# One fused attention and feed-forward kernel: the bias tables built in another way, the last tile's activations in other buffers, and every engine's queue in a new order

## The chip, the core and the metric

The kernel runs on one core of one Trainium2 chip. A core has five engines that work side by side and meet at semaphores: TensorE (PE in the profile; PEld is its weight load), VectorE (DVE), ScalarE (ACT), GpSimd (POOL) and SyncE (SP), and 16 DMA engines that move data. The metric is the time of one execution on the device in microseconds (us), as the median of several executions. Less is better.

## The reference

Attention with a bias by distance, over 8 batches, 8 heads, 576 positions and 64 channels a head, and a feed-forward layer with a leaky ReLU behind it:

```python
scores = scale * np.matmul(q, k.transpose(0, 1, 3, 2))      # 8, 8, 576, 576
bias = bias_table[bucket]                                   # 32 buckets by |i - j|, one row of 8 heads each
attn = softmax(scores + bias)                               # over the last axis
x = (attn @ v), heads side by side: 4608 rows of 512
h = x @ w_in                                                # 512 -> 2048
g = np.maximum(0.01 * h, h)
out = g @ w_out                                             # 2048 -> 512, float32
```

The bucket of a distance is the distance itself below 16, then grows with its logarithm, and is the last of the 32 from distance 128 on.

## The kernel before

**Attention.** The unit is a pair of heads of one batch, `n` = 0 to 31 (4 pairs in each of 8 batches). For a pair, q and k are turned so that channels lie on partitions (by PE from `rows`, L415 to L438, for the first pairs, later by a DMA transpose that SP issues, L424, into `tu`), and copied into `qt` and `kt` (L447). `score` (L472 to L480) multiplies them, 64 partitions a head or 128 for the leftover blocks; `expo` on ACT (L499 to L510) takes the exponential out of PSUM into `at`; `band` on DVE (L523) multiplies the band of |i - j| < 128 + 64 or so by a table of exponentials of the bias; `av` (L552, L555) multiplies by v with a column of ones, so that the row sums come with it; `norm` (L562 to L570) divides, and the result is turned back into `xT` (L576 by DMA, L584 and L589 by PE and a copy).

**The bias tables.** The exponential of the bias less that of the last bucket is a function of i - j and the head. `hk` holds it, skewed over partitions. It is made at the program's start: `hot` is a one-hot map, 32 partitions (one a bucket) by 512 distances, put together by DVE copies out of the identity matrix (L344 to L352), of which each constant run of a bucket is one copy (L348). Three more copies, each shifted by one column, stand on the other three groups of 32 partitions (`hots`, L358). `shift_table` (L361) takes the last bucket off the bias on PE, `exp_table` (L366) puts the exponentials block by block into `diag` in four ACT operations. `spread` (L374) is 16 small matmuls for each of 6 parts of the table, and `take_spread` (L377) copies each part into `hk`; `make_hk4` (L381) makes the copy for the leftover blocks. The rows of k for pair 0 come by a DMA of their own into `raw` (in the tile `y`), and ACT casts them into `pr` (L420) in one operation.

**Feed-forward.** Tokens are taken in 9 tiles `T` of 512. Tiles 0 to 2 run plain products (`ffn_in`, L603, 16 of them a tile); tiles 3 to 8 and all output products use a scheme of seven block products in place of eight. In it the input side has four units `u` a tile, each with seven products (`in_product`, L651), copies and additions into `stage` (L656 on ACT or DVE, L661 on DVE), and activations (`in_act`, L592 on ACT) that write `g`, which is [128, 16, 512] and holds one tile. `mix_g` (L687, DVE) forms sums and differences of blocks of `g`: into `gs` and, in place, into `g`. `product` (L715) is the output side, seven products of two halves `ts`, 8 matmuls each. `out_take` (L723) and `out_add` (L728) put them together in `y`, and SP stores it (L737).

There is one `g`, so the activations of a tile wait until the output products of the tile before have read it (`free_g` in `plan_seven`). In the last tile, in the order of the PE queue, products 1 and 2 are followed by product 6, which reads the block that `mix_g` 1 changes: one DVE operation over all 2048 columns.

**What sets the order.** Every step is a task with a number (`add`). `Plan.QUEUES` lists, for each engine, the numbers in the order in which they are issued, and `BANKS` the PSUM bank of each; an engine works through its own list in order and waits wherever the data is not there. Which of ACT and DVE does a copy is given by the list in which its number stands (`mover`). `FILL` puts idle matmuls on scratch data (`spin`, L1177) ahead of some tasks on PE; ten more stand at the program's start. SP and POOL issue DMAs in the order of their lists; POOL's loads of q, k, v and the weights wait for the readers of the buffer.

## Time and profile before

| | |
|---|---|
| time, median of 3 executions | 353.74 us (353.22 to 355.13) |
| the profiled execution | 354.99 us, of which the span from the first to the last instruction is 353.2 us |
| PE busy | 345.5 us, 98% of the span |
| PEld busy | 257.8 us, 73% |
| DVE busy | 298.8 us, 85% |
| ACT busy | 283.2 us, 80% |
| POOL busy | 69.4 us, 20% |
| granted TensorE clock | 1.000 mean |

How to read the lines that follow in the prediction. A row of the timeline is: start in us, duration in us, engine, line of the kernel, operation, output tile <- input tiles, partitions x elements and type, count of such instructions in a row, and in brackets the idle time of the engine just before with what ended it. Matmuls overlap, so a matmul's duration is longer than the distance to the next one; rows of the chain (the work that ended last, followed back) give the distance instead. A row of the windows gives, for a stretch of time, its length and for each engine the busy time with the number of instructions, then the granted clock, the busy share of the DMA engines and GB/s. A row of the groups gives the group, xcount, busy us, mean ns of one, and the idle time before.

### The profile page before, as it was taken

How to read it: one execution, taken by the hardware profiler on the slowest of the kernel's cores; microseconds unless marked ns; L12 is line 12 of the kernel's file. 1: busy time of each engine (PE TensorE's matmuls, PEld its weight loads, DVE VectorE, ACT ScalarE, POOL GpSimd, SP SyncE). 2: the span in 40 equal slices, each digit the busy share in tenths (PEclk: the TensorE clock that was granted, in tenths of full speed). 3: DMA queues.
4: the chain of work that ended last, by engine and by line, in shares of the span. 5: the costliest groups of instructions: out<-in, count | busy, mean ns of one | idle time of the engine just before them, and what ended most of it. 6: DMA issues, size and time to landing. Idle time of an engine off the chain costs nothing.

```text
span 353.2 us, 10334 instructions
## 1 busy us (share of the span) xinstructions
PE 345.5 (98%) x4365; PEld 257.8 (73%) x4365; DVE 298.8 (85%) x646; ACT 283.2 (80%) x436; POOL 69.4 (20%) x107
## 2 busy tenths in 40 slices
PE   8899999999999999999999999999999999999996
PEld 5666458865577556777887778688877888888875
DVE  6998599967799578998999999989988998587871
ACT  5998989589987888997987999999977981682841
...
GB/s 126 148 190 199 207 194 166 50 149 155 181 113 145 166 171 85 139 115 151 131 130 127 80 164 89 53 128 113 40 2 40 76 65 0 81 42 1 121 30 91
DMA packets 102542, 39.32 MB, mean 111 GB/s; under 512 B 82016, under 2 KB 97376, under 8 KB 102496
## 3 DMA queue, kind: packets, MB, share of 16 engines
...
q10 hardware_dynamic: 208, 0.29, 0.3%
q14 instruction: 12, 0.10, 0.1%
...
## 4 chain that ended last, share of the span: by engine, by line
PE 90%; DMA 4%; DVE 4%; ACT 1%; issue 0%; DVEq 0%; ACTq 0%
PE ps L715 29%; PE ps L651 20%; PE ps L603 12%; PE ps L552 11%; PE ps L472 9%; DMA tu<-pr 4%; PE ps L479 2%; PE ps L1177 2%; PE ps L539 1%; PE ps L492 1%; ACT g L592 1%; PE ps L433 1%; PE ps L584 1%; PE ps L438 1%; DVE g L687 1%; DVE hk L381 1%
## 5 line engine op out<-in xcount | busy, mean ns | idle before, releaser
L499 ACT ACTIVATE at<-ps 128x1024 bf16<-128x1024 f32 x124 | 123.8, 1036 | 13.1 <-PE ps L472 12.3
L715 PEld LDWEIGHTS <-g 128*128 128x128 bf16 x864 | 82.0, 98 | 16.3 <-issue 5.4
L523 DVE TENSOR_TENSOR at<-at,hk 128x768 bf16<-128x768 bf16 (+4 forms) x156 | 65.6, 447 | 9.9 <-ACT at L510 5.1
L293 POOL DMA_DIRECT2D vn<-in_v_dram x32 | 28.9, 915 | 133.6 <-PE ps L552 121.6
L715 PE MATMUL ps<-mix,g 128*128 128x256 bf16 x432 | 53.5, 273 | 0.6 <-DVE g L687 0.6
L715 PE MATMUL ps<-w_out_sb,g 128*128 128x256 bf16 x432 | 52.8, 273 | 0.0
L661 DVE TENSOR_TENSOR stage<-ps,stage 128x512 f32<-128x512 f32 x72 | 47.8, 684 | 4.8 <-PE ps L651 3.9
L552 PEld LDWEIGHTS <-at 128*128 128x128 bf16 x1240 | 42.1, 98 | 6.1 <-issue 3.5
L552 PE MATMUL ps<-vn,at 128*128 128x65 bf16 x1240 | 45.6, 194 | 0.3 <-DVE opair L563 0.3
L592 ACT ACTIVATE g<-stage 128x512 bf16<-128x512 f32 x72 | 42.5, 636 | 4.1 <-DVE stage L661 2.2
L592 ACT ACTIVATE g<-ps 128x512 bf16<-128x512 f32 x72 | 41.9, 613 | 4.0 <-PE ps L603 2.6
L603 PE MATMUL ps<-xT,w_in_sb 128*128 128x512 bf16 x192 | 45.1, 379 | 0.0
L472 PE MATMUL ps<-qt,kt 64*128 64x512 bf16 x256 | 42.8, 385 | 1.2 <-DVE qt L447 1.2
L651 PEld LDWEIGHTS <-w_in_sb 128*128 128x128 bf16 x384 | 36.0, 98 | 7.5 <-issue 2.8
L723 ACT COPY y<-ps 128x512 f32<-128x512 f32 x33 | 19.6, 594 | 23.7 <-PE ps L715 23.6
L656 ACT COPY stage<-ps 128x512 f32<-128x512 f32 x48 | 27.6, 592 | 9.9 <-PE ps L651 9.6
L603 PEld LDWEIGHTS <-w_in_sb 128*128 128x128 bf16 x192 | 17.2, 98 | 20.6 <-issue 2.4
L651 PEld LDWEIGHTS <-early 128*128 128x128 bf16 x288 | 27.2, 98 | 6.2 <-issue 2.7
L728 DVE TENSOR_TENSOR y<-ps,y 128x512 f32<-128x512 f32 (+1 forms) x29 | 18.7, 648 | 10.9 <-PE ps L715 6.0
L651 PE MATMUL ps<-early 128*128 128x256 bf16 x192 | 27.4, 273 | 0.0
L651 PE MATMUL ps<-early,w_in_sb 128*128 128x256 bf16 x192 | 27.3, 273 | 0.0
L651 PE MATMUL ps<-xT,w_in_sb 128*128 128x256 bf16 x192 | 26.7, 273 | 0.0
(107 smaller groups left out, 461.2 us busy)
## 6 DMA issues: line engine op xcount, KB each, us to landing
out_dram<-y SPq DMA_DIRECT2D x16, 512.0 KB, 3.5
...
```

The costliest lines, as they stand in the source:

```text
L293: nc.gpsimd.dma_start(out=vn[i][:, c, :, 0:D], in_=v[b, :, c * P : (c + 1) * P, :].rearrange("h s d -> s h d"),)
L472: nc.tensor.matmul(ps[:, e, :], lhsT=kt[r, u * P : (u + 1) * P], rhs=qt[r, 0:512], start=True, stop=True)
L499: nc.scalar.activation(at[:, :, u, 0:512], ps, AF.Exp, scale=scale)
L523: nc.vector.tensor_tensor(out=o, in0=o, in1=m, op=ALU.mult)
L552: nc.tensor.matmul(ps[:, ic, :], lhsT=at[:, o : o + P], rhs=vn[i][:, c, 2 * p + e, :], start=whole and c == 0, stop=not whole and ic == NJ ...
L592: nc.scalar.activation(out_, in_, AF.Prelu, bias=0.0, scale=1.0, alpha=0.01)
L603: nc.tensor.matmul(bank(("in", T, f))[:, o : o + n], lhsT=w_in_sb[:, c, f * P : (f + 1) * P], rhs=xT[:, c, x : x + n], start=(c == 0 and i ...
L651: nc.tensor.matmul(ps[:, j, :], lhsT=l, rhs=r, start=first and j == 0 and c == 0, stop=k in (2, 4, 3) and j == 1 and c == KH - 1, skip_gro ...
L656: copy(out=stage[u % 2][:, s], in_=ps)
L661: nc.vector.tensor_tensor(out=st, in0=ps, in1=st, op=ALU.add)
L715: nc.tensor.matmul(ps, lhsT=l[:, ts * P : (ts + 1) * P], rhs=r, start=k in (1, 2, 5) and (split or ts == 0) and j == 0, stop=k in (4, 2, 3 ...
L723: copy(out=y_block(k), in_=bank(("a", T)).rearrange("p (s e) -> p s e", s=2))
```

## The change

Three things change.

**The tables.** `diag` is no longer cleared and filled block by block: ACT takes one exponential over all 128 partitions into a small float32 table (`exp_table`), and DVE multiplies it by a 0/1 map of the groups (`make_diag`); the map, and the column that tells the last bucket's rows, come from two DVE reductions over the identity matrix. The far part of the one-hot map is one ACT copy over all four groups instead of DVE's 512-wide copy; the three longest runs go to ACT too. The shifted copies shrink from 511, 510 and 509 columns to 263 each and become tasks of their own (`shift_hot`), which may stand on DVE or ACT and anywhere in the queue. The cast of pair 0's raw k is split in two halves of 384 (`raw_rows`), one of which stands on ACT and one on DVE.

**The last tile.** The activations of tile 8 go into two buffers of the attention, free by then (`at_`, 8 of 16 blocks each), and wait no longer for tile 7's output products. `mix_g` 1 and 3 of that tile are split in two halves.

**The queues.** All lists in `QUEUES` and `BANKS` are new, and `FILL` holds 8 idle matmuls in place of 23.

The numbers of the tasks shift by up to seven, since there are new ones. Here the program's start on DVE, from the last runs of the one-hot map to the first copies for pair 1, before:

```order
L348 COPY stage_78<-ident 32x2x14
L348 COPY stage_78<-ident 32x2x16
L352 COPY stage_78<-stage_78 32x15
L358 COPY stage_78<-stage_78 32x511
L358 COPY stage_78<-stage_78 32x510
L358 COPY stage_78<-stage_78 32x509
L447 COPY kt_89<-ps 128x576
L451 TENSOR_TENSOR kt_89<-kt_89,own 128x128
L377 CAST hk<-ps 128x8x64 x4
L447 COPY kt_90<-ps 128x576
```

And the same place after (the changed file's lines L359, L368, L377, L398, L471 and L475 are L348, L352, L358, L377, L447 and L451 of before; L444 is half of the cast of raw k):

```order
L359 COPY stage_78<-ident 32x2x11
L367 COPY stage_78<-ident 32x16
L368 COPY stage_78<-stage_78 32x15
L373 TENSOR_REDUCE flat<-ident 128x4
L386 TENSOR_TENSOR diag<-flat 128x32
L377 COPY stage_78<-stage_78 32x263
L444 CAST pr_95<-y 96x384
L377 COPY stage_78<-stage_78 32x263 x2
L398 CAST hk<-ps 128x8x64 x4
L475 TENSOR_TENSOR kt_89<-kt_89,own 128x128
L471 COPY qt_93<-ps 128x576
```

The first copy into `kt` is gone from DVE here; it stands on ACT, behind that into `qt`. Half of the cast stands between the shifted copies.

The end of DVE's queue, tile 8, before (L687 is `mix_g`, L661 an addition of the input side, L728 one of the output side):

```order
L687 TENSOR_TENSOR gs<-g 128x1024
L661 TENSOR_TENSOR stage_78<-ps,stage_78 128x512
L661 TENSOR_TENSOR stage_77<-ps,stage_77 128x512
L661 TENSOR_TENSOR stage_78<-ps,stage_78 128x512
L687 TENSOR_TENSOR g<-g 128x4x256
L687 TENSOR_TENSOR gs<-g 128x1024
L687 TENSOR_TENSOR g<-g 128x4x256
L687 TENSOR_TENSOR g<-gs,g 128x8x256
L728 TENSOR_TENSOR y<-ps,y 128x2x256
L687 TENSOR_TENSOR g<-g 128x8x256
L728 TENSOR_TENSOR y<-ps,y 128x256 x4
```

And after, where L720 is `mix_g` and L764 `out_add`:

```order
L685 TENSOR_TENSOR stage_78<-ps,stage_78 128x512
L720 TENSOR_TENSOR at_104<-at_104 128x4x256
L720 TENSOR_TENSOR gs<-at_105 128x1024
L720 TENSOR_TENSOR at_105<-at_105 128x4x256
L720 TENSOR_TENSOR at_104<-gs,at_104 128x4x256
L720 TENSOR_TENSOR at_105<-gs,at_105 128x4x256
L764 TENSOR_TENSOR y<-ps,y 128x2x256
L720 TENSOR_TENSOR at_104<-at_104 128x4x256
L720 TENSOR_TENSOR at_105<-at_105 128x4x256
L764 TENSOR_TENSOR y<-ps,y 128x256 x4
```

The two operations over 2048 columns are now two over half of them, each on a buffer of its own.

The end of ACT's queue, from the last but four activations of tile 8 (L592) to the copies of output products (L723), before:

```order
L592 ACTIVATE g<-stage_77 128x2x256
L592 ACTIVATE g<-ps 128x2x256 x2
L592 ACTIVATE g<-stage_78 128x2x256
L592 ACTIVATE g<-stage_77 128x2x256
L592 ACTIVATE g<-stage_78 128x2x256
L723 COPY y<-ps 128x2x256 x4
```

And after (L616 and L759):

```order
L616 ACTIVATE at_105<-stage_77 128x2x256
L616 ACTIVATE at_105<-stage_78 128x2x256
L616 ACTIVATE at_105<-ps 128x2x256
L616 ACTIVATE at_105<-stage_77 128x2x256
L616 ACTIVATE at_105<-stage_78 128x2x256
L759 COPY y<-ps 128x2x256 x5
```

There are five copies where there were four: the copy of product 4 of tile 7 stands behind the first one of tile 8, because on PE both halves of that product (16 matmuls) now stand behind the last input product of tile 8. Before, they stood ahead of the last 72 matmuls of tile 8's input side.

The code's core:

```diff
     QUEUES = {
         "PE": """
-            0 18 17 27 39 37 33 31 25 47 60 61 41 43 29 23 45 90 89 68 119 66 72 76 74 105 118 97 99 95 70 54 56 103 155
...
+            0 19 20 34 28 44 48 32 36 42 65 66 95 46 30 73 94 75 38 52 106 50 110 124 79 71 123 100 81 77 59 102 61 104
...
-    FILL = {18: 5, 27: 2, 72: 1, 74: 4, 105: 5, 95: 1, 70: 5}
+    FILL = {19: 6, 50: 1, 77: 1}
...
     diag = per.tile([P, G, H], BF16, name="diag")
-    nc.vector.memset(diag, 0.0)
     hots = tables.bitcast(BF16)[:, 2 * G * NB : 2 * G * NB + UW]
     hot = hots[0:NB, :]
-    nc.vector.tensor_copy(out=hot, in_=ident[0:NB, NB - 1 : NB].to_broadcast([NB, UW]))
-    nc.vector.tensor_copy(out=hot[:, C0 : C0 + small], in_=ident[0:NB, 0:small])
+    flat = per.tile([P, 1 + G + H], FP32, name="flat")
+    is_last, group, table = flat[:, 0:1], flat[:, 1 : 1 + G], flat[:, 1 + G : 1 + G + H]
+    EDGE = BAND + G - 1
+    out_w = min(C0 - BAND, UW - 1 - C0 - BAND) + 1
+    by_group = ident.rearrange("p (g c) -> p g c", g=G)
+    nc.vector.tensor_reduce(out=is_last, in_=by_group[:, :, NB - 1], op=ALU.add, axis=mybir.AxisListType.X)
+    nc.scalar.copy(
+        out=bass.AP(tensor=hots.tensor, offset=hots.offset + C0 - BAND + 1 - out_w,
+                    ap=[list(hots.ap[0]), [2 * BAND - 1 + out_w, 2], [1, out_w]]),
+        in_=is_last.unsqueeze(1).to_broadcast([P, 2, out_w]))
+    def run_of(copy, u, lo, hi):
+        copy(
+            out=bass.AP(tensor=hot.tensor, offset=hot.offset + C0 - hi,
+                        ap=[list(hot.ap[0]), [hi + lo, 2], [1, hi - lo + 1]]),
+            in_=ident[0:NB, u : u + 1].unsqueeze(1).to_broadcast([NB, 2, hi - lo + 1]))
     for u, lo, hi in bucket_runs(NB, BAND, S):
         if lo >= small:
-            nc.vector.tensor_copy(
-                out=bass.AP(tensor=hot.tensor, offset=hot.offset + C0 - hi,
-                            ap=[list(hot.ap[0]), [hi + lo, 2], [1, hi - lo + 1]]),
-                in_=ident[0:NB, u : u + 1].unsqueeze(1).to_broadcast([NB, 2, hi - lo + 1]))
+            run_of(nc.scalar.copy if u >= NB - 4 else nc.vector.tensor_copy, u, lo, hi)
+    nc.vector.tensor_copy(out=hot[:, C0 : C0 + small], in_=ident[0:NB, 0:small])
     nc.vector.tensor_copy(
         out=hot[:, C0 - small + 1 : C0],
         in_=bass.AP(tensor=hot.tensor, offset=hot.offset + C0 + small - 1,
                     ap=[list(hot.ap[0]), [-1, small - 1]]),
     )
-    for j in range(1, G):
-        nc.vector.tensor_copy(out=hots[j * NB : (j + 1) * NB, 0 : UW - j], in_=hot[:, j:UW])
+    nc.vector.tensor_reduce(out=group, in_=by_group, op=ALU.add, axis=mybir.AxisListType.X)
+    def shift_hot(j, copy):
+        o = slice(C0 - EDGE, C0 + EDGE + 1)
+        copy(out=hots[j * NB : (j + 1) * NB, o], in_=hot[:, o.start + j : o.stop + j])
     def shift_table():
         nc.tensor.matmul(bank("d")[:, 0:H], lhsT=from_last.rearrange("b g c -> b (g c)"), rhs=tab, start=True, stop=True)
     def exp_table():
-        for j in range(G):
-            r = slice(j * NB, (j + 1) * NB)
-            nc.scalar.activation(diag[r, j, :], bank("d")[r, 0:H], AF.Exp)
+        nc.scalar.activation(table, bank("d")[:, 0:H], AF.Exp)
+    def make_diag():
+        nc.vector.tensor_tensor(out=diag, in0=table.unsqueeze(1).to_broadcast([P, G, H]),
+                                in1=group.unsqueeze(2).to_broadcast([P, G, H]), op=ALU.mult)
...
-        src = raw.rearrange("r e (c d) -> r e c d", d=D) if n == 0 else \
-            (qn, kn)[j][b % NBUF][0:RQ, 2 * p : 2 * p + 2, :, :]
-        (nc.scalar.copy if n == 0 else nc.vector.tensor_copy)(out=prs[n % NPR][:, j, :, :].rearrange("r c (e d) -> r c e d", e=2),
-                        in_=src.rearrange("r e c d -> r c e d"))
+        nc.vector.tensor_copy(out=prs[n % NPR][:, j, :, :].rearrange("r c (e d) -> r c e d", e=2),
+                              in_=(qn, kn)[j][b % NBUF][0:RQ, 2 * p : 2 * p + 2, :, :].rearrange("r e c d -> r c e d"))
+    def raw_rows(h, copy):
+        o = slice(h * NC // 2, (h + 1) * NC // 2)
+        copy(out=prs[0][:, 1, o, :].rearrange("r c (e d) -> r c e d", e=2),
+             in_=raw.rearrange("r e (c d) -> r e c d", d=D)[:, :, o, :].rearrange("r e c d -> r c e d"))
...
     def in_act(T, u, i, r, s=None):
-        o = g[:, 4 * u + 2 * i : 4 * u + 2 * i + 2, r * HT : (r + 1) * HT]
+        part, f = g_part(T, 4 * u + 2 * i)
+        o = part[:, f : f + 2, r * HT : (r + 1) * HT]
         prelu(o, stage[u % 2][:, s] if s is not None else bank(("X", T, u)).rearrange("p (j t) -> p j t", j=2))
...
-    def g_block(r, h, lo=0, hi=NK):
-        return g.rearrange("p (j h) t -> p j h t", h=2)[:, lo:hi, h, r * HT : (r + 1) * HT]
-    def mix_g(k, lo, hi):
-        a11, a12, a21, a22 = [g_block(r, h, lo, hi) for r in range(2) for h in range(2)]
+    g_last = [at_[i][:, 0 : n_fc // 2 * TT].rearrange("p (f t) -> p f t", t=TT) for i in range(2)]
+    def g_part(T, f):
+        return (g, f) if T < n_tt - 1 else (g_last[2 * f // n_fc], f % (n_fc // 2))
+    def g_block(T, r, h, lo, hi):
+        part, f = g_part(T, 2 * lo)
+        return part.rearrange("p (j h) t -> p j h t", h=2)[:, f // 2 : f // 2 + hi - lo, h, r * HT : (r + 1) * HT]
+    def mix_g(T, k, lo, hi):
+        a11, a12, a21, a22 = [g_block(T, r, h, lo, hi) for r in range(2) for h in range(2)]
         s1 = gs[:, lo:hi, :]
         out_, in0, in1, op = ((s1, a21, a22, ALU.add), (a11, s1, a11, ALU.subtract),
                               (a21, a11, a21, ALU.subtract), (a12, a12, a11, ALU.subtract))[k]
         nc.vector.tensor_tensor(out=out_, in0=in0, in1=in1, op=op)
...
     sh = add("PE", 0.3, [tabl], shift_table, -99, take=[("d", 1)])
-    e8t = add("ACT", 0.8, [sh], exp_table, -99, give=[("d", 1)])
+    e8t = add("ACT", 0.25, [sh], exp_table, -101, give=[("d", 1)])
+    e8t = add("DVE", 0.12, [e8t, dma(4.1)], make_diag, -99)
+    shifts = []
     hkt, hk4t = [], []
     def plan_table():
+        for j in range(1, G):
+            t = add("DVE", 0.3, [dma(4.1)], lambda j=j: shift_hot(j, mover(shifts[j - 1])), -98)
+            t["other"] = ("ACT", 0.4)
+            shifts.append(t)
         t = e8t
         for m in range(BW // JB):
-            t = add("PE", 0.46, [e8t, dma(5.9)], lambda m=m: spread(m), -20, soft=[t] + (rowt[0][-1:] if m > 1 else []) + hkt[m - 2 : m - 1],
+            t = add("PE", 0.46, [e8t] + shifts, lambda m=m: spread(m), -20, soft=[t] + (rowt[0][-1:] if m > 1 else []) + hkt[m - 2 : m - 1],
                     take=[(("u", m), 1)])
             hkt.append(add("DVE", 0.61, [t], lambda m=m: take_spread(m), -20, soft=hkt[-1:] + (cut[0][1:2] if m > 0 else []),
                            give=[(("u", m), 1)]))
...
-            r0, r1 = L["raw", 0], add("ACT", 0.75, [L["raw", 1]], lambda: rows(0, 1), -100)
+            r0, r1 = L["raw", 0], []
+            for h in range(2):
+                t = add(("ACT", "DVE")[h], 0.45, [L["raw", 1]] + [dma(4.1)] * h, lambda h=h: raw_rows(h, mover(r1[h])), -100)
+                t["other"] = (("DVE", "ACT")[h], 0.45)
+                r1.append(t)
...
-        free_g = outs_of.get(T - 1, [])
+        free_g = outs_of.get(T - 1, []) if T < n_tt - 1 else []
...
-        sm[1] = add("DVE", 1.13, ps[1] + [sm[k, lo] for k in (0, 2) for lo in (0, NK // 2)], lambda: mix_g(1, 0, NK), 1)
+        parts = ((0, NK // 2), (NK // 2, NK)) if final else ((0, NK),)
+        sm[1] = [add("DVE", 1.13 / len(parts) + 0.04, ps[1] + [sm[k, x] for k in (0, 2) for x in (0, NK // 2)],
+                     lambda lo=lo, hi=hi: mix_g(T, 1, lo, hi), 1) for lo, hi in parts]
         prod(2, 1, of(0, 0, NK, 1), [Bk])
         d11 = add("DVE", 0.61, ps[2] + [c11], lambda: out_add(T, "b", 0), 4, give=[Bk])
-        sm[3] = add("DVE", 1.13, ps[2] + [sm[1]], lambda: mix_g(3, 0, NK), 3)
-        prod(6, 2, [c11, sm[1]])
+        sm[3] = [add("DVE", 1.13 / len(parts) + 0.04, ps[2] + sm[1], lambda lo=lo, hi=hi: mix_g(T, 3, lo, hi), 3) for lo, hi in parts]
+        prod(6, 2, [c11] + sm[1])
```

56 lines of the change are left out of this document (29 added, 27 removed), and 130 rows, old and new, of the table QUEUES.

## The prediction

> **What bounds the kernel now.** I read the page's summary first, then the windows, to see which engine is full where.
>
> ```profile
> PE 345.5 (98%) x4365; PEld 257.8 (73%) x4365; DVE 298.8 (85%) x646; ACT 283.2 (80%) x436; POOL 69.4 (20%) x107
> ...
> 24.00:28.00 4.00, 4.00 (x98) 2.98 (x95) 3.90 (x14) 3.98 (x5) 1.46 (x2) 1.00 2.27 163
> 28.00:32.00 4.00, 3.66 (x78) 2.98 (x76) 3.32 (x12) 3.95 (x7) 2.45 (x3) 1.00 1.34 198
> ...
> 240.00:260.00 20.00, 20.00 (x265) 15.98 (x262) 19.50 (x40) 18.88 (x31) 0.00 (x0) 1.00 0.33 53
> ...
> 340.00:360.00 20.00, 9.35 (x85) 7.89 (x82) 4.36 (x7) 1.75 (x3) 0.00 (x0) 0.99 0.16 53
> ```
>
> PE is busy everywhere, but matmuls overlap, so that says little; the chain of waits gives the distance from one to the next.
>
> ```profile
> 97.21 0.87 PE ps L715 x8
> 98.08 0.76 PE ps L472 x6
> 98.84 0.98 PE ps L715 x8
> ```
>
> Eight output matmuls take 0.87, which is 0.109 each; right behind scores the same eight take 0.98. So a change from the 64-partition form of the scores back to 128 costs 0.11. Three pairs of scores at 0.22 (a 512-wide matmul, 0.216) would take 0.65 and take 0.76: the change into that form costs as much. From 33 us to the end the chain is such pieces back to back, so there every us of PE work or PE waiting is a us of time. PE's work is the same after the change, except for the idle matmuls. What can change is how early PE is full, how often it changes form, and how long it waits. There are three stretches.
>
> *The start.* The first columns are start and duration.
>
> ```profile
> 3.25 0.63 POOL L285 DMA_DIRECT2D kn<-in_k_dram  x1
> ...
> 4.15 0.83 ACT L420 CAST pr<-y 96x768 bf16<-96x768 f32 x1 [1.45 <-DMA y<-in_k_dram]
> ...
> 4.49 0.63 POOL L285 DMA_DIRECT2D kn<-in_k_dram  x1
> ...
> 5.15 1.26 DVE L358 COPY stage<-stage 32x511 bf16<-32x511 bf16 x3
> ...
> 5.62 0.69 PE L438 MATMUL ps<-ident,qn 96*64 96x96 bf16 x12
> ...
> 6.36 0.64 ACT L447 COPY qt<-ps 128x576 bf16<-128x576 bf16 x1 [0.77 <-PE ps L438]
> 6.44 0.76 DVE L447 COPY kt<-ps 128x576 bf16<-128x576 bf16 x1
> 6.47 0.70 PEld L374 LDWEIGHTS <-stage 128*128 128x128 bf16 x16
> ...
> 7.26 1.04 PE L472 MATMUL ps<-qt,kt 64*128 64x512 bf16 x4
> ...
> 7.91 1.94 ACT L499 ACTIVATE at<-ps 128x1024 bf16<-128x1024 f32 x2 [0.91 <-PE ps L472]
> ```
>
> The first scores start at 7.26, when both copies are there. DVE comes to its copy of k when it is through with the table, at 6.41. From 7.91 on ACT has exponentials, and the windows from 24 to 32 us show ACT and DVE both nearly full (3.98 and 3.90 of 4): it is they that say when the four pairs of the first batch are through and the feed-forward matmuls, PE's filling, can begin:
>
> ```profile
> 28.80 0.67 ACT L506 ACTIVATE at<-ps 128x576 bf16<-128x576 f32 x1
> ...
> 31.39 0.18 DVE L562 RECIPROCAL rcp<-ps 128x4 f32<-128x4 f32 x1 [0.61 <-PE ps L555]
> ...
> 33.07 0.81 PE L603 MATMUL ps<-xT,w_in_sb 128*128 128x512 bf16 x3
> 33.12 0.17 DVE L562 RECIPROCAL rcp<-ps 128x1 f32<-128x1 f32 x1 [0.41 <-PE ps L552]
> ```
>
> *The middle* has one long wait:
>
> ```profile
> 147.23 13.97 DMA tu<-pr
> ...
> 161.23 0.36 DVE L420 COPY pr<-qn 96x768 bf16<-96x768 bf16 x1 [1.76 <-DMA tu<-pr]
> ...
> 163.39 0.60 PE L651 MATMUL ps<-xT,early 128*128 128x256 bf16 x4 [0.64 <-DVE stage L661]
> ```
>
> A DMA transpose took 13.97 in a burst of loads. DVE stood 1.76 before it could write the transpose's source anew, and PE stood for an addition behind that: its matmul before that wait was issued at 162.56, and such a one (64 wide) takes 0.03, so PE lost 163.39 - 162.56 - 0.03 = 0.80.
>
> *The end:*
>
> ```profile
> 327.66 1.67 ACT L592 ACTIVATE g<-stage 128x512 bf16<-128x512 f32 x3 [0.40 <-PE ps L715]
> ...
> 336.20 0.60 PE L651 MATMUL ps<-xT,early 128*128 128x256 bf16 x4 [0.17 <-DVE stage L661]
> ...
> 336.56 1.68 ACT L592 ACTIVATE g<-stage 128x512 bf16<-128x512 f32 x3
> 336.79 3.65 PE L715 MATMUL ps<-w_out_sb,g 128*128 128x256 bf16 x32
> ...
> 338.27 0.69 DVE L687 TENSOR_TENSOR gs<-g 128x1024 bf16<-128x1024 bf16 x1
> ...
> 339.00 0.69 DVE L687 TENSOR_TENSOR g<-g 128x1024 bf16<-128x1024 bf16 x1
> ...
> 339.79 1.23 DVE L687 TENSOR_TENSOR g<-gs,g 128x2048 bf16<-128x2048 bf16 x1
> ...
> 341.07 1.92 PE L715 MATMUL ps<-mix,g 128*128 128x256 bf16 x16 [0.63 <-DVE g L687]
> ```
>
> After the last input product PE has only the 32 matmuls of products 1 and 2 of tile 8 (3.49 at 0.109). They end their turn at 336.79 + 3.49 = 340.28, and PE waits until 341.07, 0.79, for the 2048-wide mix. A shorter wait stands ahead: 336.20 shows a matmul 0.33 later than the chain's pace, and the first output matmul follows 0.16 late.
>
> **The change, part by part.** *The table.* DVE loses the clearing of `diag`, the 512-wide copy, and three long runs; it gains two reductions and a small product. The three shifted copies (1.26 in all) become three of half the width. These operations are short: DVE's row shows what they are worth, about 0.07 for a run, 0.29 for a shifted copy and 0.65 for the first of them, which stood behind POOL's work:
>
> ```profile
> L358 DVE COPY stage<-stage x3: 289/290/654, 5.2 to 6.1; 32x511 bf16<-32x511 bf16 x1, 32x510 bf16<-32x510 bf16 x1, 32x509 bf16<-32x509 bf16 x1
> ```
>
> I put the saving on DVE at 0.5 to 0.7, but half of the cast of k (0.83 / 2, about 0.45) comes onto DVE between the shifted copies. So the table is through at about 6.2, not 6.41. The gain would be larger if the first scores waited for nothing else. They do: both first copies are now on ACT, one behind the other; q's transposes come first (six idle matmuls at 0.21 after 3.87, then 0.69 to about 5.8), k's to about 6.2 and its copy to 6.8; and on PE 32 `spread` matmuls, which need all shifted copies, stand ahead of the first score. Sixteen of them took 0.70, so 32 from 6.2 on end at 7.1 or so with a pace near 0.03. The first score thus starts at 7.0 to 7.25: a gain of 0.1, at most 0.25. If the tables slip by more than 0.1, there is none.
>
> [...]
>
> *The first batch's queue.* ACT up to the last exponential that tile 0 needs: 16 large ones, 4 of 576 and 3 of 512 columns in both queues, with 4 copies before and 3 after. That is 0.6 less (a copy is 0.64), and 0.1 for the first score: 0.7 off ACT's path. DVE up to the copy that completes tile 0: 5 copies of q and k where there were 6 (-0.7), one more band (+0.5) and one more small product (+0.2), 0.2 for the earlier end of the table: 0.2 off. What DVE waited near the end (0.61 and 0.41 in the rows) may shrink or not. From 0.2 and 0.7 and these waits I take 0.8 earlier for the first L603. PE has done more by then: the new queue puts four pieces of scores of pairs 4 and 5 and the turning of pair 3 ahead of the first L603, the old one three and not the turning. One score piece is 0.22 + 0.22 and the turning about 0.2 (four matmuls, at 0.056 each): 0.4 to 0.6 of work, I take 0.4. Term: -1.2; from 0 (the tables slip, the waits stay) to -2.2 (all the 1.0 of waits go).
>
> The 15 idle matmuls that go stood in PE's waits and cost nothing; ACT and DVE hide them.
>
> *The middle.* Counted in the two queues from the first L603 on, PE changes form 130 times before and 126 after: 4 x 0.1 = -0.4. The wait for the transpose (0.80) and two small ones of 0.16 behind it, 1.1 in all, go if the burst falls otherwise: between the rows of pair 21 and the rows of pair 23, which overwrite them, DVE has 27 tasks in both queues. Over pairs 9 to 29 that room grew for 14 and shrank for 6, but from the rows of pairs 30 and 31 to the copies of what their transposes bring there are 12 and 7 tasks where there were 35 and 37. Each new wait of that kind costs 0 to 1.1. I take half of the 1.1: -0.5, from -1.1 to +1.0. The loads themselves stand in the same order on POOL, the clearing of the edges (six small memsets) now behind pair 4's q and k.
>
> *The end.* Tile 8's activations need not wait for tile 7's reading of `g`; that wait was on ACT (0.40 in the row at 327.66) and PE was full then, so it is worth nothing by itself. Its worth is that PE can hold back tile 7's product 4, 16 matmuls or 1.75, until the last input product of tile 8 is done. Count from that point: DVE's chain was through 341.02 - 336.52 = 4.5 later, PE reaches product 6 after 1.75 + 3.49 = 5.2. The 0.79 and the 0.16 go, with 0.7 to spare, and the split of the 1.23 into two halves makes the first half free 0.6 sooner. The wait of 0.33 inside the input products has the same order around it after the change, so I leave it. If the cover is gone (DVE later by over 0.7), PE waits for what is over. The copy of product 4 now stands behind that of tile 8's product 1 on ACT, and tile 7's store behind that; tile 8's copy into the same quarter of `y` comes three products later (5.2), and a store of this size took 3.5, so it is not late. Term: -1.0, from -0.8 to -1.3.
>
> ```profile
> out_dram<-y SPq DMA_DIRECT2D x16, 512.0 KB, 3.5
> ```
>
> What follows the last matmul, an addition and the stores, is the same.
>
> **Sum.** -1.2 - 0.4 - 0.5 - 1.0 = -3.1 on the profiled execution: a span of 353.2 - 3.1 = 350.1. That execution took 354.99, 1.8 over its span, and lies 1.25 above the median of 353.74; the terms are differences inside the span, so they come off the median: 353.74 - 3.1 = 350.6.
>
> **The rivals.** *The start hands nothing on* (same). The spreads ahead of the first score and the half cast on DVE eat the gain, and DVE's 0.2 is all that its path gives. Speaks for it: DVE is as full as ACT in the windows, and its list hardly gets shorter. Against: the late DVE waits, and PE's work done earlier. Then also one new wait in the middle: 0 - 0.4 + 0 - 1.0 = -1.4, 352.3.
>
> *DVE stands before DMA transposes* (same, a little slower at worst). DVE's list is in order, and where its copy comes soon after the rows that feed the transpose, a landing time like 13.97 stops it; each wait of 1.76 cost PE about 1.1. For: pairs 30 and 31 have less room than before; DVE is at 19.50 of 20 there. Against: no POOL loads in that stretch (0 busy), and the DMA share is 0.33 of 16. Two more such waits than before and the old one kept: +2.2 - 0.4 - 1.2 - 1.0 = -0.4, 353.3; from four more on it is slower than before.
>
> *The clock falls in the start* (slower). With 15 idle matmuls fewer, PE has longer pauses between 10 and 33 us, and its granted clock, which the page shows at full for all slices, could fall by half. The ten first matmuls show the slow pace, 0.21 each, beside 0.109:
>
> ```profile
> 1.10 2.31 PE L1177 MATMUL ps<-stage 128*128 128x256 bf16 x10 [1.10 <-DVE stage L319]
> ...
> L472 PE MATMUL ps<-qt,kt 64*128 64x512 bf16 x34 | 6.0, 383 | 1.2 <-DVE qt L447 1.2
> L552 PE MATMUL ps<-vn,at 128*128 128x65 bf16 x119 | 5.1, 194 | 0.3 <-DVE opair L563 0.3
> ```
>
> Between 10 and 33 us, the 17 pairs of scores of its row would each take 0.22 more (3.7) and the 119 narrow ones 0.03 (3.6). PE's own pauses, the 1.2 of the row and about 0.3 in the window from 28 to 32, take up some 2 of the 7.3. If the clock stays down for all of it: 350.6 + 5.3 = 355.9. It decides only if the clock is down for most of the 23 us. Against: PE once issued nothing for 1.2 us (the wait of the L472 row) and the clock stayed. [...]
>
> **How the numbers follow.** 0.5% of 353.74, about what a measurement of this kernel can tell from no change, is 1.8. Forecast: 0.69, faster. Nothing handed on: 0.14, same. Transposes: 0.13, of which 0.10 same and 0.03 slower. Clock: 0.04, slower. So faster 0.69, same 0.24, slower 0.07. Range: the best ends of the terms give -2.2 - 0.4 - 1.1 - 1.3 = -5.0, 348.7; the worst give 0 - 0.4 + 1.0 - 0.8 = -0.2, 353.5. Both ends at once are unlikely; I cut 0.2 below and keep the upper end, since two rivals lie there: 348.9 to 353.5.
>
> **What would show it.** First score at 7.0 to 7.25 and the first feed-forward matmul near 32.3, with one score piece more ahead of it. No wait of PE between the input products of tile 8 and its product 6, and DVE's two halves through before PE gets there. No DVE wait of over 1 us for a transpose between 140 and 260 us. I am wrong if the first feed-forward matmul starts after 33, if the granted clock shows a digit under 9 past 10 us, or if PE's waits between 40 and 330 us sum to more than before.

## The result, and the profile after

The changed kernel takes 352.03 us (median; 351.60 to 352.73), measured beside the kernel before at 354.08 us: a ratio of 0.9941 with a 95% interval from 0.9914 to 0.9967. Measured once more, beside runs C, E and G: 352.09 beside 353.51, 0.9955 (0.9938 to 0.9972). So it is faster by 1.4 to 2.1 us; the forecast was 3.1. The profiled execution took 352.14, with a span of 350.4, 2.8 below that of before.

The summary of the page after, and the windows that were shown of before:

```profile
PE 343.0 (98%) x4350; PEld 256.5 (73%) x4350; DVE 295.5 (84%) x643; ACT 284.1 (81%) x441; POOL 69.7 (20%) x107
```

```profile
24.00:28.00 4.00, 4.00 (x70) 2.58 (x67) 3.97 (x13) 4.00 (x7) 1.43 (x2) 1.00 2.31 156
28.00:32.00 4.00, 2.98 (x76) 2.54 (x75) 2.91 (x12) 3.38 (x6) 2.45 (x3) 1.00 1.45 191
240.00:260.00 20.00, 20.00 (x282) 15.32 (x280) 18.45 (x40) 18.53 (x30) 0.00 (x0) 1.00 0.28 68
...
340.00:360.00 20.00, 7.12 (x66) 6.15 (x63) 1.98 (x5) 1.75 (x3) 0.00 (x0) 0.95 0.16 54
```

PE has 2.2 us less to do behind 340: its work ends earlier. But from 28 to 32 us PE is busy for 2.98 of 4, where it was 3.66: the start looks worse, not better. The start in the timeline:

```profile
3.50 1.02 DVE L359 COPY stage<-ident 32x6 bf16<-32x6 bf16 x12 [0.47 <-ACT stage L353]
...
5.05 0.19 DVE L386 TENSOR_TENSOR diag<-flat 128x32 bf16<-128x32 f32 x1
...
5.25 0.48 DVE L377 COPY stage<-stage 32x263 bf16<-32x263 bf16 x1
...
5.77 0.55 DVE L444 CAST pr<-y 96x384 bf16<-96x384 f32 x1
...
6.35 0.64 DVE L377 COPY stage<-stage 32x263 bf16<-32x263 bf16 x2
...
7.05 0.96 PE L395 MATMUL ps<-diag,stage 128*128 128x32 bf16 x32 [0.24 <-DVE stage L377]
...
7.94 0.61 PE L496 MATMUL ps<-qt,kt 64*128 64x512 bf16 x4
...
8.38 1.94 ACT L523 ACTIVATE at<-ps 128x1024 bf16<-128x1024 f32 x2 [0.90 <-PE ps L496]
...
33.49 0.81 PE L627 MATMUL ps<-xT,w_in_sb 128*128 128x512 bf16 x3
```

DVE waits 0.47 for ScalarE's wide copy, since both write the one-hot map, and comes to its first shifted copy at 5.25 (5.15 before). The three copies take 1.12 (0.48, 0.40 and 0.23) with the half cast of 0.55 between them; the table is through at 6.99 (6.41 before). The first scores start at 7.94 (7.26), the first exponential at 8.38 (7.91), the first feed-forward matmul at 33.49 (33.07).

The tail in the timeline:

```profile
332.99 1.91 PE L751 MATMUL ps<-mix,g 128*128 128x256 bf16 x16
...
334.74 3.66 PE L751 MATMUL ps<-w_out_sb,at 128*128 128x256 bf16 x32
...
336.50 1.29 DVE L720 TENSOR_TENSOR at<-gs,at 128x1024 bf16<-128x1024 bf16 x2
...
338.23 1.91 PE L751 MATMUL ps<-mix,at 128*128 128x256 bf16 x16
```

Behind the last input product come 16 matmuls of tile 7, then 32, then product 6 at 338.23 without a wait; DVE is through with both halves at 337.79.

**Where the time went.** To compare executions I put them on PE's own work. Each matmul counts with its distance to the next at full pace (0.109 for 256 columns, 0.216 for 512, and so on; idle ones count nothing), and a column tells how much later than in the profiled execution of before a kernel had issued the same amount of work. The head gives the time in before. A change of form of the matmuls shows as a step of 0.1 that passes, so differences under 0.2 say little.

| us against before | at 25.9 | 46.0 | 160.8 | 168.1 | 291.7 | last matmul |
|---|---|---|---|---|---|---|
| changed kernel | -0.92 | +0.06 | +0.24 | -0.90 | -1.35 | -2.86 |
| changed kernel, second profile | -0.36 | +0.08 | -0.03 | -1.06 | -1.62 | -3.13 |
| A first scores later | -0.16 | +0.16 | +0.06 | -1.08 | -1.53 | -3.04 |
| B scores ahead of the table | +1.41 | +1.59 | +1.50 | +0.35 | -0.09 | -1.60 |
| C cast on ScalarE | -1.07 | -0.59 | -0.69 | -1.72 | -2.28 | -3.79 |
| D tail undone | -0.42 | -0.09 | +1.14 | +0.00 | -0.45 | -1.02 |
| E before, tail alone | -0.47 | -0.29 | -0.30 | -1.31 | -1.45 | -1.30 |
| F before, middle reordered | -1.09 | -1.02 | -1.02 | -1.54 | -1.54 | -1.54 |
| G before, no idle matmuls | +1.63 | +1.98 | +2.14 | +1.13 | +0.99 | +0.99 |
| H before, narrow idle matmuls | +1.61 | +1.22 | +1.22 | +0.71 | +0.56 | +0.56 |
| I changed, no idle matmuls | +0.66 | +0.75 | +0.65 | -0.38 | -0.92 | -2.43 |
| J | -1.30 | -1.17 | -1.27 | -2.30 | -2.84 | -4.35 |
| K | -1.04 | -0.96 | -1.06 | -2.09 | -2.63 | -4.14 |

The changed kernel gains nothing by 46 us, 1.1 in one place at 161 to 168, 0.3 on the rest of the way, and 1.5 behind 291.7.

### The profile page after: what moved, and what is told of

Its sections match the earlier page's. It is cut to its first block, busy times and chain, and to the rows that moved or that the text cites. A ratio compares the mean times of both kernels' runs of the same rounds, so it can differ in the third digit from the quotient of the medians.

```text
span 350.4 us, 10314 instructions
## 1 busy us (share of the span) xinstructions
PE 343.0 (98%) x4350; PEld 256.5 (73%) x4350; DVE 295.5 (84%) x643; ACT 284.1 (81%) x441; POOL 69.7 (20%) x107
## 4 chain that ended last, share of the span: by engine, by line
PE 89%; DVE 4%; ACT 4%; DMA 2%; issue 1%; POOL 0%; DVEq 0%; POOLq 0%
PE ps L751 31%; PE ps L675 21%; PE ps L576 11%; PE ps L627 11%; PE ps L496 8%; ACT at L523 2%; PE ps L503 2%; DMA tu<-pr 2%; PE ps L563 1%; PE ps L516 1%; ACT early L523 1%; PE ps L608 1%; DVE g L720 1%; PE ps L457 1%; DVE opair L594 0%
## 5 line engine op out<-in xcount | busy, mean ns | idle before, releaser
L751 PEld LDWEIGHTS <-g 128*128 128x128 bf16 x768 | 72.1, 98 | 15.5 <-issue 5.6
L751 PE MATMUL ps<-mix,g 128*128 128x256 bf16 x384 | 47.7, 273 | 0.1
L751 PE MATMUL ps<-w_out_sb,g 128*128 128x256 bf16 x384 | 46.9, 273 | 0.0
L496 PE MATMUL ps<-qt,kt 64*128 64x512 bf16 x256 | 41.9, 381 | 0.5 <-ACT at L523 0.2
L616 ACT ACTIVATE g<-ps 128x512 bf16<-128x512 f32 x68 | 38.5, 621 | 1.3 <-PE ps L627 1.0
L680 ACT COPY stage<-ps 128x512 f32<-128x512 f32 x51 | 29.1, 589 | 12.1 <-PE ps L675 11.8
L616 ACT ACTIVATE g<-stage 128x512 bf16<-128x512 f32 x60 | 35.0, 632 | 4.2 <-DVE stage L685 4.2
L759 ACT COPY y<-ps 128x512 f32<-128x512 f32 x30 | 17.7, 594 | 13.2 <-PE ps L751 13.2
L764 DVE TENSOR_TENSOR y<-ps,y 128x512 f32<-128x512 f32 (+1 forms) x29 | 18.7, 649 | 9.2 <-ACT y L759 4.9
```

The costliest lines, as they stand in the source:

```text
L496: nc.tensor.matmul(ps[:, e, :], lhsT=kt[r, u * P : (u + 1) * P], rhs=qt[r, 0:512], start=True, stop=True)
L616: nc.scalar.activation(out_, in_, AF.Prelu, bias=0.0, scale=1.0, alpha=0.01)
L680: copy(out=stage[u % 2][:, s], in_=ps)
L751: nc.tensor.matmul(ps, lhsT=l[:, ts * P : (ts + 1) * P], rhs=r, start=k in (1, 2, 5) and (split or ts == 0) and j == 0, stop=k in (4, 2, 3 ...
L764: nc.vector.tensor_tensor(out=o, in0=ps, in1=o, op=ALU.add)
```

## The experiments

My theory after the result: the tail is the gain; the start gained nothing because its first exponential came later, and ScalarE, which in the timeline after has no pause from 8.38 to 30.9, hands such a shift on. The rival: the start hands nothing on at all. Beside runs A, B, D and F the kernel before took 353.32 us; beside C, E, G and the second measurement of the changed kernel 353.51; beside H to K 353.79.

**A. The first scores later.**

```diff
     nc.vector.tensor_reduce(out=group, in_=by_group, op=ALU.add, axis=mybir.AxisListType.X)
+    nc.vector.tensor_reduce(out=group, in_=by_group, op=ALU.add, axis=mybir.AxisListType.X)
+    nc.vector.tensor_reduce(out=group, in_=by_group, op=ALU.add, axis=mybir.AxisListType.X)
```

> The changed kernel with one small DVE reduction of the start (0.27 us, into the group map) done three times in place of once, so that DVE comes 0.54 us later to all that follows: the table, half of k's cast, and so the first scores. Theory A (ScalarE works without a pause from its first exponential at 8.38 to 30.9, so the start is bounded by it and every shift of the first exponential is handed on): first exponential near 8.9, first feed-forward matmul near 34.0 (33.49 in the changed kernel), time 0.4 to 0.6 above the changed kernel. Rival B (the start hands nothing on in either direction, because DVE's divisions and the PSUM banks they free set the pace at 29 to 33): first feed-forward matmul within 0.2 of 33.49, time within 0.2 of the changed kernel.

Measured: 352.51 us, 0.9970 (0.9955 to 0.9985), 0.4 to 0.5 above the changed kernel's medians, but the intervals overlap (0.9938 to 0.9972 for that one). The first exponential and the first feed-forward matmul:

```profile
9.08 1.94 ACT L525 ACTIVATE at<-ps 128x1024 bf16<-128x1024 f32 x2 [0.97 <-PE ps L498]
...
33.59 0.81 PE L629 MATMUL ps<-xT,w_in_sb 128*128 128x512 bf16 x3
```

The time speaks for theory A, the row at 33.59 for rival B. The trace shows why they differ: at 25.9 us PE's work stands 0.76 later than in the first profile of the changed kernel, which then loses 0.69 in one wait that this run lacks. In the changed kernel:

```profile
29.57 0.26 PE L576 MATMUL ps<-vn,at 128*128 128x65 bf16 x3
30.35 0.20 PE L576 MATMUL ps<-vn,at 128*128 128x65 bf16 x1 [0.53 <-issue]
```

"issue" means that nothing which the profile shows ends the wait. A by itself decides nothing; G takes the wait up.

**B. Scores ahead of the table.** Task 17 is DVE's half of the cast, 2 the product for `diag`, 25 a shifted copy; 44 and 48 are scores, 34 and 28 pieces of the table. Two PSUM banks change with them.

```diff
-PE  0 19 20 34 28 44 48 32 ...
+PE  0 19 20 44 48 34 28 32 ...
-DVE 2 25 17 26 27 ...
+DVE 17 2 25 26 27 ...
```

> The changed kernel with two orders of the start changed: DVE does its half of the cast of k first, ahead of the product for diag and the first shifted copy; and PE does the first two pieces of scores ahead of the first two pieces of the table. First scores should come at 7.2 to 7.4 (7.94 in the changed kernel) and the first exponential near 7.7 (8.38). Theory A (ScalarE bounds the start, every shift is handed on): first feed-forward matmul near 32.8, time 0.5 to 0.7 below the changed kernel, near 351.4. Rival B (nothing is handed on): within 0.2 of the changed kernel. Between the two: the copies out of the table's pieces on DVE now come 0.2 to 0.5 later, which could give back part of it.

Measured: 352.83 us, 0.9983 (0.9968 to 0.9998): 0.7 to 0.8 slower than the changed kernel, although the first exponential came at 7.92.

```profile
9.37 2.48 DVE L398 CAST hk<-ps 128x512 bf16<-128x512 f32 x4 [3.15 <-PE ps L395]
...
11.29 1.02 ACT L523 ACTIVATE at<-ps 128x1024 bf16<-128x1024 f32 x1 [1.44 <-PE ps L496]
```

DVE now gets the table's pieces at 9.37 in place of 8.12, and ScalarE waits 1.44 for the next scores. Neither theory had this right: an early first exponential is worth nothing when the next ones have to wait. How much of the +1.4 at 25.9 us is the order isn't shown: in this profile PE's 512-wide matmuls also keep a slow pace, 0.60 to 0.63 each, up to 15 us, where the first profile of the changed kernel has 0.39 from 7.94 on. The +1.5 at 46 us is there to the end (+1.50 at 160.8 us, and 1.3 behind the changed kernel at the last matmul), so from 46 us on nearly all of a loss is handed on.

**C. Both halves of the cast on ScalarE.** It stood idle from 4.5 to 5.9 us.

```diff
-ACT 1 18 21 22 ...
+ACT 1 18 17 21 22 ...
-DVE 2 25 17 26 27 ...
+DVE 2 25 26 27 ...
```

> The changed kernel with DVE's half of the cast of k given to ScalarE, behind the other half (ScalarE is idle there), so that DVE is through with the shifted copies 0.55 earlier and k's turning comes 0.7 earlier: first scores near 7.4 (7.94), first exponential near 7.9 (8.38), and the table's pieces 0.5 earlier too. Theory A (ScalarE bounds the start and hands its shift on): first feed-forward matmul near 33.0, time 0.4 to 0.5 below the changed kernel. Theory C (what PE waits for at 29 to 30 us is its own instructions, which come no earlier): PE comes to its 478th matmul near 29.1 and waits there to about 30.3, first feed-forward matmul within 0.2 of 33.5, time within 0.2 of the changed kernel.

Measured: 351.10 us, 0.9934 (0.9916 to 0.9952), 1.0 below the changed kernel beside it.

```profile
5.27 0.95 DVE L377 COPY stage<-stage 32x263 bf16<-32x263 bf16 x3
...
6.34 1.05 PE L395 MATMUL ps<-diag,stage 128*128 128x32 bf16 x32
...
7.33 1.04 PE L496 MATMUL ps<-qt,kt 64*128 64x512 bf16 x4
...
7.98 1.94 ACT L523 ACTIVATE at<-ps 128x1024 bf16<-128x1024 f32 x2 [0.76 <-PE ps L496]
...
32.84 0.81 PE L627 MATMUL ps<-xT,w_in_sb 128*128 128x512 bf16 x2
```

The table and the scores are 0.6 to 0.8 earlier, the first exponential 0.4, and 0.7 stays from 25.9 us to the last matmul (table, against the second profile; 0.9 at the end against the first). That is more than the 0.4 to 0.5 that were expected. Theory A holds in direction and theory C falls: PE lost only 0.2 behind the 478th matmul. So a start that is earlier as a whole is handed on, and the half cast on DVE held it back. That a shift of the first exponential alone is handed on one to one isn't shown.

**The changed kernel once more.**

> The changed kernel once more, unchanged, so that the three kernels beside it have it on the same chip, and for a second profile of its start. Both theories of the start: about 0.994 of the kernel before. If PE's wait of 0.69 at 29.6 us in the first profile, which ends with nothing that the profile shows, belongs to a place in PE's instruction stream, it stands at the same matmul again (the 478th pair of weight load and matmul), unless PE comes there later than about 30.4 us.

Measured: 352.09 us, 0.9955 (0.9938 to 0.9972). The wait stands behind the same matmul, the 478th, but PE comes there at 30.1 in place of 29.6 and loses 0.2 in place of 0.69. What is new is in the windows, the column ahead of the last two:

```profile
8.00:10.00 2.00, 2.00 (x39) 1.10 (x38) 1.80 (x3) 1.55 (x2) 2.00 (x4) 0.54 1.11 142
10.00:12.00 2.00, 2.00 (x40) 1.50 (x38) 1.86 (x6) 1.92 (x3) 2.00 (x4) 0.61 2.13 154
```

The granted clock is down for about 3.4 us, an estimate from the two shares at 0.50 while it is down (the value that H shows). In the first profile it was 1.00 there, which was worth 0.7 at 12 us and nothing at 46.

**D. The tail undone.** 1640 and 1641 are product 4 of tile 7, 1687 and the like input products of tile 8, 1725 product 1 of tile 8.

```diff
-PE ... 1676 1644 1664 ... 1715 1640 1641 1725 ...
+PE ... 1676 1640 1641 1644 1664 ... 1715 1725 ...
```

> The changed kernel with one thing of the tail undone: on PE, product 4 of tile 7 (two halves, 16 matmuls) stands ahead of the last stretch of input products of tile 8 again, in place of behind the last of them. Buffers, halves of the mixes and all other lists are as in the changed kernel. Theory (the held-back product is the cover): DVE's two halves of the mix end 4.2 and 4.8 us behind the last input product in the changed kernel's trace, PE has 3.49 of work until product 6, so PE waits 0.7 to 0.9 there and the time is 0.7 to 0.9 above the changed kernel. Rival (the two buffers alone free the tail, since the activations come earlier and DVE with them): no wait, time within 0.2 of the changed kernel.

Measured: 352.98 us, 0.9985 (0.9973 to 0.9997), 0.9 above the changed kernel.

```profile
335.64 0.93 PE L751 MATMUL ps<-w_out_sb,at 128*128 128x256 bf16 x7
...
336.80 2.90 PE L751 MATMUL ps<-w_out_sb,at 128*128 128x256 bf16 x25 [0.24 <-ACT at L616]
...
339.89 2.08 PE L751 MATMUL ps<-mix,at 128*128 128x256 bf16 x16 [0.19 <-DVE at L720]
```

PE loses 0.40 in front of the eighth matmul (for an activation), 0.36 in front of product 6 and 0.17 inside it: 0.93, as the table has it (0.94 behind 291.7). The held-back product is the cover. (The +1.2 between 46 and 160.8 is a wait at 71 us in this one execution, far from the edit.)

**E. The tail alone, in the kernel before.** Buffers, halves and PE's order of the tail as in the change; numbers of before:

```diff
-PE  ... 1631 1635 1636 1639 1640 ... 1710 1720 ...
+PE  ... 1631 1639 1640 ... 1710 1635 1636 1720 ...
-ACT ... 1637 ... 1722 1730 ...
+ACT ... 1722 1637 1730 ...
-SP  ... 1642 1643 ...
+SP  ... 1643 1642 ...
```

> The kernel before with the last tile's part of the change alone: activations of tile 8 in the two buffers of the attention, the two mixes in halves, and on PE product 4 of tile 7 behind the last input product of tile 8 (its copy on ScalarE behind the first copy of tile 8, the two stores of tile 7 in the other order, two PSUM banks changed for it). All else as before. Theory (the tail is a part by itself, and the largest): PE's 0.33, 0.16 and 0.79 of waiting go, time 1.2 to 1.6 below the kernel before. The prediction's term was 1.0, without the 0.33. Rival (the tail's gain needs the new lists elsewhere, since DVE and ScalarE come into the tail as before): 0 to 0.5.

Measured: 353.82 us, 1.0004 (0.9986 to 1.0022): no gain. The theory's number is far off, the rival's holds. PE's waits of 0.16 and 0.79 are gone, the one of 0.33 is still there, and a new one has come:

```profile
322.41 1.04 PE L724 MATMUL ps<-w_out_sb,gs 128*128 128x256 bf16 x8
...
324.23 1.91 PE L724 MATMUL ps<-w_out_sb,g 128*128 128x256 bf16 x16 [0.78 <-DVE y L737]
```

Product 4 had covered something else: it stood between products 5 and 3 of tile 7, and product 3 needs an addition on DVE that follows 5. With it gone PE stands idle for 0.78 there, and is 0.94 behind its pace. The new lists put four input products at that place (322.07 to 323.82 in the changed kernel), and PE has no wait there. That these are the other half of the tail's gain is argued from this; no run puts them alone into the kernel before.

**F. The middle.** 668 copies the rows of pair 23 over the source of the slow transpose; 616 and 617 are the copies of q and of k that this transpose brings for pair 21; 1146 and 1170 are the additions that PE waited for.

```diff
-DVE ... 1148 668 616 1146 1170 669 ... 1155 617 1195 ...
+DVE ... 1148 616 1146 1170 668 617 669 ... 1155 1195 ...
```

> The kernel before with one thing changed in the middle of DVE's list: two tasks that depend on the slow transpose (the rows of pair 23, and the copy of what the transpose brings for pair 21) stand behind the two additions of tile 3's input products, where they stood ahead. Theory (the transpose of 13.97 us costs time only because DVE's order hands its wait to PE): PE's wait of 0.80 and the two small ones behind it go, time 0.8 to 1.1 below the kernel before. Rival 1 (the wait falls on the next task that PE needs): within 0.3 of the kernel before, with a wait of DVE nearby. Rival 2 (the slow transpose is a matter of one execution and is not there in most): within 0.3 of the kernel before, and no long transpose in the profile.

Measured: 354.14 us, 1.0013 (0.9995 to 1.0031): no gain. But the edit is not quite what the expectation says. Of the tasks that need the transpose only 668 went behind the additions; 616, which needs it as much, still stands ahead of them, and 617, which stood further back, came forward. The transpose is nearly as slow in this profile (12.9 us to its landing), DVE now waits 0.6 for it ahead of 616, and PE still loses 0.41 at 163.7 us and twice 0.16 behind that. So this run does not tell the theory from rival 1, and the sign of rival 2, no long transpose in the profile, is not there.

Other runs help. E, G and H have DVE's list of before at this place. On the way from 160.8 to 168.1 us E and G gain the same 1.0 on the kernel before as the changed kernel does, H and F half of it. What waits for the transposes in F, in E, and in the changed kernel:

```profile
  DVE qt L447: 0.6, 1
...
DMA to landing us min/median/max: 3.2/4.4/12.9
```

```profile
  DVE pr L417: 0.3, 1
...
DMA to landing us min/median/max: 3.3/3.9/12.5
```

```profile
  DVE pr L439: 1.2, 1
...
DMA to landing us min/median/max: 3.3/4.3/13.0
```

Long transposes are in all of them. With the old list DVE's wait for the one at this place was 1.76 in before, 1.08 in H, 0.3 in E and none in G, so what it costs PE changes with the execution, from 1.1 to nothing. In the changed kernel DVE met a transpose at 96 us, and PE lost nothing by it.

**G. The kernel before without its 23 idle matmuls.**

```diff
-    FILL = {18: 5, 27: 2, 72: 1, 74: 4, 105: 5, 95: 1, 70: 5}
+    FILL = {}
```

> The kernel before without the 23 idle matmuls that its lists put ahead of tasks at 4 to 20 us (the ten at the very start stay). As predicted, they stand in PE's waits and cost nothing: time within 0.2 of the kernel before, first feed-forward matmul within 0.2. Rival 1 (PE's instruction stream comes too slowly there, and 46 instructions less let it come 23 matmuls further by the time it waits for code): 0.3 to 0.7 below. Rival 2 (the clock falls without them): a digit under 9 in the clock's row between 5 and 33 us, and 1 us or more above.

Measured: 355.27 us, 1.0046 (1.0029 to 1.0062): 1.8 slower. Not free at all.

```profile
24.58 0.28 PE L552 MATMUL ps<-vn,at 128*128 128x65 bf16 x4
...
26.24 0.19 PE L555 MATMUL ps<-v,at 128*128 128x65 bf16 x1 [1.38 <-issue]
```

PE stops for 1.54 behind its 350th matmul, and for 0.79 behind the 478th. The latter is the place of the wait of 0.69 in the changed kernel, with other work there. Between the two lie 128 weight loads and 128 matmuls. The trace has 34 packets of 16,384 bytes on an instruction queue, about one for each such stretch of PE's 4342 matmuls. The DMA view of one us, of before (19 to 20) and of this run (23 to 24), shows the packet for the stretch behind the 350th:

```profile
q8 instruction: 1, 0.02, 6.0%
```

```profile
q8 instruction: 1, 0.02, 6.0%
```

It starts at 19.53 in before and at 23.67 here, and PE comes to the place at 23.7 and at 24.7; it goes on 1.6 us after the packet's end here. Behind the 478th matmul it goes on 1.5 us after the end of such a packet in the changed kernel, and 1.4 in the kernel before, which loses 0.50 there. So I read it that PE waits for its own code; the profile names no releaser. That is the cause which rival 1 named, but it expected a gain, and the run is slower.

**H. Idle matmuls of 16 columns in place of 256.**

```diff
-    def spin(k):
+    def spin(k, w=16):
         for _ in range(k):
-            nc.tensor.matmul(pw, lhsT=junk[:, 0:P], rhs=junk[:, 0:256], start=True, stop=True)
+            nc.tensor.matmul(pw[:, 0:w], lhsT=junk[:, 0:P], rhs=junk[:, 0:w], start=True, stop=True)
-    spin(10)
+    spin(10, 256)
```

> The kernel before with its 23 idle matmuls 16 columns wide in place of 256 (as many instructions, almost no work on PE). Theory (what the idle matmuls give is their place in PE's instruction stream: without them the 16 KB of code that PE needs at its 350th matmul was fetched from 23.67 us on, with them from 19.53): code comes as in the kernel before, no wait of over 0.3 us at the 350th matmul, time within 0.3 of the kernel before. Rival (it is their work that counts, keeping PE busy or spacing its requests): as without them, 1.2 to 2.0 above the kernel before, with a wait of over 1 us at the 350th matmul.

Measured: 354.55 us, 1.0018 (0.9998 to 1.0037), 0.8 above before, where the theory had 0.3 at most. As expected for the code: its packet starts at 19.2, and no wait stands behind the 350th matmul. But +1.2 stands at 46 us in this profile, from another place, where the clock is down (the column ahead of the last two):

```profile
16.00:18.00 2.00, 1.42 (x21) 0.89 (x22) 2.00 (x5) 2.00 (x5) 1.58 (x5) 0.74 1.57 189
18.00:20.00 2.00, 2.00 (x21) 0.59 (x16) 1.86 (x7) 1.62 (x3) 1.72 (x3) 0.50 1.14 194
20.00:22.00 2.00, 2.00 (x32) 1.54 (x32) 1.12 (x3) 2.00 (x3) 2.00 (x4) 0.50 1.14 207
```

So as instructions the idle matmuls bring the code early (the packet at 19.2, at 23.67 in G). As work they seem to hold the clock in these lists: its mean is 0.990 to 0.995 in 7 of the 12 executions here and in 5 of the 9 of G, but in 3 of the 25 of the kernel before beside this run. That is not the whole of the 0.8: the five executions of H with a clock of 0.999 or more have a median of 354.42, which is still 0.6 above before. Where that comes from, and how the request for code is set off, the runs don't show.

**I. The changed kernel without the eight that it kept** (`FILL = {}`).

> The changed kernel without the 8 idle matmuls that it kept (six at 3.9 us, one at 14.3, one at 18.0). Theory (instruction stream): if the request for the code of the 350th matmul slips as it did in the kernel before without its 23, PE waits 0.5 to 1.6 there and the time is 0.5 to 1.6 above the changed kernel; if the request stays before 21 us, nothing. Rival (they only fill waits): within 0.2 of the changed kernel whenever the request starts.

Measured: 352.80 us, 0.9969 (0.9947 to 0.9992), 0.7 above the changed kernel. The packet starts at 22.9, PE loses 0.70 behind the 350th matmul:

```profile
24.50 0.20 PE L576 MATMUL ps<-vn,at 128*128 128x65 bf16 x1
25.23 0.27 PE L576 MATMUL ps<-vn,at 128*128 128x65 bf16 x3 [0.53 <-issue]
```

The theory holds for the wait; the interval of the time overlaps with the changed kernel's. Eight are enough to bring the packet at 19.8. That the fifteen which the change drops cost nothing fits this, but no run puts them back. The clock is 0.998 or more in all executions of this run, so in the new lists nothing shows that idle matmuls hold it.

**J and K. Better versions.** J is C with the reduction for the last bucket's rows ahead of `from_last` on DVE. K adds one step on PE: 171, scores of pair 4, ahead of 153, products by v.

```diff
-    nc.vector.tensor_tensor(out=from_last, ...)
     nc.vector.tensor_reduce(out=is_last, ...)
+    nc.vector.tensor_tensor(out=from_last, ...)
-PE  ... 147 177 153 121 155 171 201 ...
+PE  ... 147 177 171 153 121 155 201 ...
```

> The version with both halves of the cast of k on ScalarE, and also the reduction that tells the last bucket's rows ahead of the 0.28 product that makes from_last on DVE, so that ScalarE's wide copy and DVE's runs behind it come 0.2 earlier. If a shift of the first exponential is handed on one to one: 0.1 to 0.2 below the version without it, 0.8 to 0.9 below the changed kernel. Rival (the next thing, q's load that lands at 5.0 us, holds the first score where it is): the same as the version without it, 0.6 to 0.7 below the changed kernel.

> As the one above, and one piece of scores of pair 4 on PE ahead of the small piece of products by v at 31.2 us, where PE waits 0.68 in every run of the changed kernel's lists for a division on DVE to free a PSUM bank. Theory (the piece, 0.32 with its change of form, fills the wait): 0.3 to 0.4 below the one above. Rival (the wait moves: the products come later and with them the tile's turning and the first feed-forward matmul): within 0.1.

Measured: J 351.25 us, 0.9927 (0.9899 to 0.9955); K 350.53 us, 0.9902 (0.9872 to 0.9931), the fastest of all: 3.3 below before, 1.5 below the changed kernel. K's waiting place, after which the first feed-forward matmul starts:

```profile
30.82 0.39 PE L496 MATMUL ps<-qt,kt 64*128 64x512 bf16 x2 [0.19 <-ACT at L523]
31.15 0.29 PE L576 MATMUL ps<-vn,at 128*128 128x65 bf16 x4
...
32.48 0.81 PE L627 MATMUL ps<-xT,w_in_sb 128*128 128x512 bf16 x2
```

In J the products by v start at 30.69, 0.68 behind the matmul ahead of them. In K they start at 31.15, 0.71 behind that matmul (30.44), but with 0.22 of scores in between; the rest is a wait for an exponential and changes of form. So the piece fills a third of the place, not all of it. Between C, J and K the intervals overlap: neither that J is better than C (351.25 against 351.10) nor that K is better than J is shown.

## Why the prediction was right, and where it was wrong

The direction was right and the time lies in the range. That the sum came out nearly whole in the spans (2.8 of 3.1) is luck: its errors cancel.

- *The table, "through at about 6.2"*: failed. 6.99. The half cast was counted (0.45, was 0.55); what was saved ahead of the shifted copies went into a wait that the prediction did not look for, 0.47 for ScalarE's write to the same tile, and a reduction and a product of 0.46 together. Half the width saved little: an undisturbed copy took 0.23 in place of 0.29, and two of the three took 0.48 and 0.40.
- *"Term: -1.2" for the start*: failed, 0 or worse. Its premise that an earlier start is handed on was right (C); the shift had the other sign (the first exponential +0.47, the first feed-forward matmul at 33.49, past the 33 that the prediction gave as a sign of being wrong). ScalarE took the shift back, with fewer copies and without the pauses of 0.36 and 0.15 that it had before: +0.06 at 46 us. Against two other profiles of the old start (E -0.29, F -1.02) the new start is 0.3 to 1.1 later there. The rival "the start hands nothing on" gave 352.3 and named the half cast and the spreads; it was the better description.
- *"The 15 idle matmuls that go ... cost nothing"*: nothing speaks against the result, but the reason was wrong. The old 23 did not just stand in PE's waits: without them PE stands for 1.54 and 0.79, which I put down to its code, and the time is 1.8 longer (G), and without the eight that are left PE waits 0.70 (I).
- *Form changes, -0.4*: between 46 and 291.7 the changed kernel gains 1.4, of which 1.1 is at the place of the transpose's wait; the 0.3 left fits, but wasn't tested alone.
- *Middle, -0.5*: in the profiles -1.1. The wait comes and goes with the execution (F), so what the new lists gain there lies between 0 and 1.1, and how often is open. The profiled execution of before lay 1.25 over its median, and the prediction took its terms off the median as if every execution had them; that fits most of the gap between 3.1 foreseen and 1.4 to 2.1 measured. No DVE wait of over 1 us for a transpose came from 140 to 260 us, as foreseen.
- *End, -1.0*: right in mechanism, 1.5 in size. D puts 0.94 of it on the held-back product; the waits of 0.33 and 0.16 went too, and did not come back in D. "0.7 to spare" was 0.44 (337.79 to 338.23), so the halves of the mix decide nothing: an undivided 1.23 would be in time as well. What the step missed is what product 4 had covered before (E).
- *Clock rival*: its price was too high. The clock does fall between 8 and 12 us in some executions of the new start (second profile 0.54 and 0.61, D 0.63 and 0.52, in windows of 2 us), for about 3.4 us, and nothing of it is left at 46. It is not the change's alone: the kernel before beside H to K has a mean clock of 0.995 in 3 of 25 executions. The profile page's clock row, "full for all slices", also hides a slow start: in before the 512-wide matmuls took 0.59 to 0.63 up to 9.5 us. That longer pauses bring the fall is not shown: in the second profile PE's longest pause from 3.87 us to the fall was 0.91 (between the transposes of q and of k), and in before PE stood for 1.19 ahead of 15.81 while the clock stayed at 1.00. What the runs show is that it falls more often in the old lists when the idle matmuls are narrow or gone: 7 of 12 executions of H, 5 of 9 of G.
- *"0.65 for the first of them, which stood behind POOL's work"*: that POOL's work is the cause is not shown. It is the first of the shifted copies that is slow: 0.47 to 0.54 where it starts at 5.23 to 5.27, with half of the cast on DVE (0.48, changed kernel) or without it (0.47 in C, 0.54 in J), and 0.22 to 0.23 where it starts at 5.52 (B) or 5.91 (A). POOL clears a part of `v` from 5.11 to 5.66 in before, A, B and C. The copy of B starts within that time and is not slow, and no run moves POOL's operation. The half cast took 0.53 to 0.55 on DVE and 0.50 to 0.51 on ScalarE.
